# Decode attention with a gated unit on one core: keys and probabilities turned by VectorE instead of TensorE, softmax per key tile

## The chip, the cores and the metric

The kernel runs on 1 core of a Trainium2 chip. The metric is the device time of one execution in microseconds (us), lower is better. The engines named below are PE (TensorE: matmuls; PEld is its weight load), DVE (VectorE), ACT (ScalarE), POOL (GpSimd) and SP (SyncE, which here only issues DMAs).

## The reference

One decoding step of a block for 8 sequences (B = 8, one token each, D = 512). All tensors are bf16.

```python
xn = layernorm(x)                                   # 8 x 512
q  = (xn @ wq) -> 32 heads of 128
k  = k_cache[:, :, 8192-2048:, :]                   # 8 kv heads, window W = 2048
v  = v_cache[:, :, 8192-2048:, :]                   # each kv head serves 4 query heads
s  = softmax(q . k * 128**-0.5) . v   -> 8 x 4096,  then @ wo   -> 8 x 512
g  = silu((sigmoid(xn @ w_gate) * (xn @ w_up)) @ w_down)        # F = 1792
out = x + s * g
```

The window of keys and values is 2 x 32 MB, the weights are some 14 MB: 81 MB to read.

## The kernel before

**Tiles and loads.** A key or value tile holds 4 kv heads of one sequence: 128 partitions x 64 positions x 128 numbers, 2 MB. Each partition holds 64 neighbouring positions of one head, and the partitions go round the four heads (partition 4p + l has head l). There are 16 key tiles and 16 value tiles (sequence b, half i of the heads). All loads go through SP's queue in a fixed list: the weights of the gated unit and wq, then key tile n and value tile n - 3 in turn, at last wo in five pieces. `pump` issues the next load of the list as soon as its pool (`room`: 5 key buffers, 4 value buffers) has room in the program's order; SP itself waits until the buffer's last reader is done. wq and wo use key buffers, the gated unit's weights value buffers.

**Before the loop.** Layernorm, the gated unit's two products, q (`q_ps` L344), the gated unit's last product, and some selector tiles built from identities by POOL and DVE. `qm_sb` holds q turned, 4 query rows of one kv head in 32 columns that are otherwise zero; `M0` and the offset `o` in `scores` shift them so that one head's scores land on rows of their own.

**The loop**, over sequences b and 16 half steps s each, an order written out by hand (`tasks`): `k_transposes` (L488) turns the keys 128x128 at a time by matmuls with a permutation, which also sorts the heads, into PSUM, 16 to a group, and DVE copies each group to SBUF (L493, kT_sb). `scores` (L505) multiplies four heads side by side, each in its own 32 columns of the PE array. Once for a sequence, one step behind: `row_max`, `stat_rows`, `spread_max` find the maximum of each head over its rows (a DVE maximum, a PE transpose to one row, two small DVE operations, a PE transpose back) and take the exponentials into `p_buf`; `p_transposes` (L599) turns the probabilities on PE and DVE copies them (L590). Two sequences behind, `values` (L625) multiplies them with the value tiles; `combine`, `heads`, `divide` merge the parts of each head and divide by the sums.

**The tail.** The last two sequences' probabilities and values, then the product with wo (`part_ps` L754, `fin_ps` L768), the gate, the sum with x, and the store.

Of the kernel before, what the change touches and what calls it, by code (L numbers as in the profile page):

```python
# [10 lines left out]
def kernel(  # L11
# [13 lines left out]
    nc = tc.nc  # L25
# [17 lines left out]
    CH = CU // 2  # L43
    NU = NQ * NJ
    NR = NU * rep
# [9 lines left out]

    padpool = ctx.enter_context(tc.tile_pool(name="padpool", bufs=1))
    padpool.tile([P, 96], f32, name="pad")
    kpool = ctx.enter_context(tc.tile_pool(name="kpool", bufs=5))
    vpool = ctx.enter_context(tc.tile_pool(name="vpool", bufs=4))
    ktpool = ctx.enter_context(tc.tile_pool(name="ktpool", bufs=3))  # L60
    ppool = ctx.enter_context(tc.tile_pool(name="ppool", bufs=2))
# [23 lines left out]
    room = {"k": 5, "v": 4, "d": 1}  # L85
# [127 lines left out]
    for t0, t1 in ((0, 12), (12, KS), (KS, 26), (26, 30), (30, RT)):  # L213
        want_rows("wo_sb", A_wo, "k", RT, t0, t1)

    pump()

    perm = consts.tile([P, P], bf16, name="perm")
    nc.gpsimd.tensor_copy(
        out=perm[:].rearrange("k (l p) -> k l p", l=G),  # L220
        in_=ident[:].rearrange("k (p l) -> k l p", l=G),
    )

# [34 lines left out]
    M0 = Z - rep  # L258
    qm_sb = work.tile([P, B, Hkv, M0 + Z], bf16, name="qm_sb")
    nc.gpsimd.memzero(qm_sb[:])  # L260
    p_buf = [work.tile([P, PG, G, CU], bf16, name=f"p_buf{i}") for i in range(2)]
    for t in p_buf:
        nc.gpsimd.memzero(t[:])
# [75 lines left out]
    q_ps = [ps_s.tile([P, rep * Dh], f32, name="q_ps", tag="s") for _ in range(2)]  # L339
    for kt in range(KT):  # L340
        for x in range(Hkv // JQ):
            for j in range(JQ):
                g = x * JQ + j
                nc.tensor.matmul(  # L344
                    q_ps[x][Z * j : Z * (j + 1), :],
                    lhsT=xnT_sb[:, kt, :],
                    rhs=weights[("wq_sb", kt)][:, g * rep * Dh : (g + 1) * rep * Dh],
                    start=(kt == 0),
                    stop=(kt == KT - 1),
                    tile_position=(0, Z * j),  # L350
                    skip_group_check=True,
                )
    q_bf = ktpool.tile([P, 2, rep, Dh], bf16, name="q_bf", tag="kT")
    qT_ps = ps_t.tile([P, 2, rep, P], bf16, name="qT_ps", tag="t")
    for x in range(Hkv // JQ):
        src = q_ps[x][:].rearrange("k (r d) -> k r d", r=rep)
        nc.scalar.copy(out=q_bf[:, x], in_=src)
    for x in range(Hkv // JQ):
        for r in range(rep):
            nc.tensor.transpose(  # L360
                out=qT_ps[:, x, r, :], in_=q_bf[:, x, r, :], identity=ident[:]
            )
        nc.vector.tensor_copy(  # L363
            out=qm_sb[:, :, x * JQ : (x + 1) * JQ, M0 : M0 + rep],
            in_=qT_ps[:, x].rearrange("d r (j z) -> d z j r", z=Z)[:, ::S],
        )
# [25 lines left out]
    w_ps = ps_s.tile([P, D], f32, name="w_ps", tag="s")  # L392
# [13 lines left out]
    b_ps = ps_s.tile([P, P], f32, name="b_ps", tag="s")  # L406
# [16 lines left out]
    Hh = G * rep  # L423
    turn_rows = consts.tile([P, P], bf16, name="turn_rows")
    sel_den = consts.tile([P, Hq], f32, name="sel_den")
    sel_out = consts.tile([P, 2, Hq], f32, name="sel_out")
    for i in range(NQ):
        nc.gpsimd.tensor_copy(
            out=turn_rows[:].rearrange("k (i j l r) -> k i j l r", i=NQ, j=NJ, l=G)[
                :, i  # L430
            ],
            in_=ident[:].rearrange("k (l j i r) -> k i j l r", i=NQ, j=NJ, l=G)[:, i],
        )
        nc.vector.reduce_sum(
            out=sel_den[:, i * Hh : (i + 1) * Hh].rearrange("k (l r) -> k l r", l=G),
            in_=ident_f[:].rearrange("k (l j i r) -> k i l r j", l=G, j=NJ, i=NQ)[:, i],
            axis=AX.X,
        )
    for e in range(2):
# [19 lines left out]
    sel_sum = consts.tile([P, Hq, NDQ], f32, name="sel_sum")  # L459
    nc.gpsimd.tensor_copy(  # L460
        out=sel_sum[:], in_=sel_den[:].unsqueeze(2).to_broadcast([P, Hq, NDQ])
    )
# [8 lines left out]
    kT_ps = {}  # L471
# [10 lines left out]
    def k_transposes(b, u, h):  # L482
        i, j = u // NJ, u % NJ
        k_sb = k_tiles[(b, i)]
        if h == 0:
            kT_ps[0] = ps_t.tile([P, CU, P], bf16, name="kT_ps", tag="t")
        for c in range(h * CH, (h + 1) * CH):
            nc.tensor.transpose(  # L488
                out=kT_ps[0][:, c, :], in_=k_sb[:, j * CU + c, :], identity=perm[:]
            )  # L490
        if h == 1:
            kT[(b, u)] = ktpool.tile([P, CU, P], bf16, name="kT_sb", tag="kT")
            nc.vector.tensor_copy(out=kT[(b, u)][:], in_=kT_ps.pop(0)[:])  # L493
        if j == NJ - 1 and h == 1:
            del k_tiles[(b, i)]
            free("k")

    def scores(b, u):
        i, j = u // NJ, u % NJ
        if u == 0:  # L500
            s_ps[b] = ps_s.tile([P, CU * PG], f32, name="s_ps", tag="s")
        t = kT.pop((b, u))
        o = M0 - rep * (j * NQ + i)
        for l in range(G):
            nc.tensor.matmul(  # L505
                s_ps[b][NR * l : NR * (l + 1), :],
                lhsT=qm_sb[:, b, i * G + l, o : o + Z],
                rhs=t[:, :, PG * l : PG * (l + 1)],
                start=(u == 0),
                stop=(u == NU - 1),  # L510
                tile_position=(0, NR * l),
                skip_group_check=True,
            )


    NH = NQ * rep

    def row_max(b):
        st[b] = small.tile([P, 1], f32, name="st")
        nc.vector.reduce_max(out=st[b][:], in_=s_ps[b][:], axis=AX.X)  # L520

    def stat_rows(b):
        nc.tensor.transpose(out=r_ps[b % 2], in_=st.pop(b)[:], identity=ident_f[:])
        top = small.tile([1, G, NH], f32, name="top")
        nc.vector.reduce_max(
            out=top[:],
            in_=r_ps[b % 2].rearrange("o (l j h) -> o l h j", l=G, j=NJ),
            axis=AX.X,
        )
        row[b] = small.tile([1, G, NJ, NH], f32, name="neg")  # L530
        nc.vector.tensor_scalar(
            out=row[b][:],
            in0=top[:].unsqueeze(2).to_broadcast([1, G, NJ, NH]),
# [5 lines left out]
    def spread_max(b):  # L539
        nc.tensor.transpose(  # L540
            out=nb_ps[b % 2],
            in_=row.pop(b)[:].rearrange("o l j h -> o (l j h)"),
# [3 lines left out]
        nc.scalar.copy(out=nb[:], in_=nb_ps[b % 2])  # L546

        s = s_ps.pop(b)
        if b % 2 == 0:
            sums_of[b // 2] = small.tile([P, 2], f32, name="sums")  # L550
        if b == B - 1:
            e_sb = ktpool.tile([P, PG, CU], bf16, name="e_sb", tag="kT")
            nc.scalar.activation(  # L553
                out=e_sb[:],
                in_=s[:].rearrange("k (c p) -> k p c", p=PG),
                func=AF.Exp,
                bias=nb[:],
                scale=scale,
                accum_out=sums_of[b // 2][:, b % 2 : b % 2 + 1],
            )  # L560
            move = (
                nc.vector.tensor_copy,
                nc.gpsimd.tensor_copy,
                nc.scalar.copy,
                nc.vector.tensor_copy,
            )
            for l in range(G):
                rows = slice(NR * l, NR * (l + 1))
                move[l](out=p_buf[b % 2][rows, :, l, :], in_=e_sb[rows])  # L569
            return  # L570
        for l in range(G):
            rows = slice(NR * l, NR * (l + 1))
            nc.scalar.activation(  # L573
                out=p_buf[b % 2][rows, :, l, :],
                in_=s[rows, :].rearrange("k (c p) -> k p c", p=PG),
                func=AF.Exp,
                bias=nb[rows, :],
                scale=scale,
                accum_out=sums_of[b // 2][rows, b % 2 : b % 2 + 1],
            )  # L580

    pT_ps = {}

    def p_transposes(b):
        p_turn(b, 0)
        p_turn(b, 1)
        p_copy(b, 0, CU, nc.vector.tensor_copy)

    def p_copy(b, c0, c1, copy):
        copy(out=pT[b][:, c0:c1, :], in_=pT_ps[b][:, c0:c1, :])  # L590
        if c1 == CU:
            del pT_ps[b]

    def p_turn(b, h):
        if h == 0:
            pT[b] = ppool.tile([P, CU, P], bf16, name="pT_sb")
            pT_ps[b] = ps_t.tile([P, CU, P], bf16, name="pT_ps", tag="t")
        for c in range(h * CH, (h + 1) * CH):
            nc.tensor.transpose(  # L599
                out=pT_ps[b][:, c, :],  # L600
                in_=p_buf[b % 2][:, :, :, c].rearrange("k p l -> k (p l)"),
                identity=turn_rows[:],
            )


# [214 lines left out]
```

## Time and profile before

| what | value |
|---|---|
| median of 3 runs | 199.63 us (199.42 to 200.01) |
| profiled execution | 199.11 us, its span 197.3 us |
| granted PE clock, mean over the span | 0.972 |
| DMA | 81.32 MB, mean 412 GB/s, 16 engines busy at 9 tenths or more from the second slice to the last but two |
| key transposes L488 on PE | x1024, 76.5 us |
| their copies L493 on DVE | x64, 78.2 us, mean 1222 ns |
| value matmuls L625 | x512, 38.7 us |
| score matmuls L505 | x256, 25.9 us |
| exponentials L573 on ACT | x28, 19.0 us, mean 679 ns, each with an accumulator read of 184 ns |

The profile is of one execution. Its span runs from the first to the last instruction, and the execution took 1.8 us more. Busy times of PE are modelled at their ends, since matmuls are pipelined. The chain that ended last is followed back from the last instruction to what released each step.

### The profile page before, as it was taken

The page shows a single profiled execution, that of the slowest core. Times are in us where ns is not written, and L with a number is a line of the kernel's source. Part 1 is how long each engine was busy: PE and PEld are TensorE (multiplying, and loading weights), DVE is VectorE, ACT ScalarE, POOL GpSimd, SP SyncE. Part 2 cuts the span into 40 slices and gives each one's busy share as a digit, 9 for nine tenths or more (in the row PEclk, how much of TensorE's full clock was granted, in tenths as well). Part 3 has the DMA queues.
Part 4 walks back from the last instruction along what each step waited for, and adds up shares of the span by engine and source line. Part 5 has one row for each costly group of instructions (what it writes and reads, how often), then busy time and mean ns, then how long its engine had stood idle before and what let it go on. Part 6 is the DMA issues. An engine that isn't in the chain of part 4 may idle for free.

```text
span 197.3 us, 4706 instructions
## 1 busy us (share of the span) xinstructions
PE 155.2 (79%) x2138; PEld 105.4 (53%) x2138; DVE 114.9 (58%) x144; ACT 35.8 (18%) x87; POOL 13.8 (7%) x32
## 2 busy tenths in 40 slices
PE   0073575999799996999798979796989797749763
PEld 0021124777586675667565746474658464538521
DVE  4624002889877574657794766476848664764311
ACT  0510210000900600060006001500050024032110
POOL 8960001000000000000000000000000000010000
PEclk9999999999999998899999999999999999999975
DMA  6999999999999999999999999999999999999980
GB/s 212 436 438 438 423 431 422 432 435 425 428 428 435 423 428 428 442 422 425 425 432 423 432 432 425 435 428 428 432 428 425 425 428 432 438 428 424 407 372 29
DMA packets 6436, 81.32 MB, mean 412 GB/s; under 512 B 777, under 2 KB 785, under 8 KB 1553
## 3 DMA queue, kind: packets, MB, share of 16 engines
q1 hardware_dynamic: 6237, 80.10, 95.3%
q10 hardware_dynamic: 180, 0.93, 1.4%
q8 instruction: 16, 0.26, 0.5%
q14 instruction: 3, 0.02, 0.0%
HBM read 81.02 MB, written 0.01 MB: 411 GB/s over the span
## 4 chain that ended last, share of the span: by engine, by line
DMA 75%; PE 20%; SPq 1%; DVE 1%; issue 0%; ACT 0%; DVEq 0%
DMA k_sb<-in_A_k_cache_dram 62%; PE kT_ps L488 11%; DMA wo_sb<-in_A_wo_dram 10%; PE o_ps L625 4%; DMA wg_sb<-in_B_w_gate_dram 3%; PE s_ps L505 3%; PE fin_ps L768 1%; PE pT_ps L599 1%; SPq L90 1%; DVE kT_sb L493 1%; PE part_ps L754 1%; ACT part L764 0%; SPq L100 0%; SPq L150 0%; DVE prod L783 0%
## 5 line engine op out<-in xcount | busy, mean ns | idle before, releaser
L493 DVE COPY kT_sb<-kT_ps 128x2048 bf16<-128x2048 bf16 x64 | 78.2, 1222 | 37.0 <-PE kT_ps L488 36.6
L488 PE MATMUL kT_ps<-perm,k_sb 128*128 128x128 bf16 x1024 | 76.5, 225 | 12.3 <-DMA k_sb<-in_A_k_cache_dram 12.2
L488 PEld LDWEIGHTS <-k_sb 128*128 128x128 bf16 x1024 | 60.5, 100 | 32.5 <-issue 16.3
L625 PE MATMUL o_ps<-v_sb,pT_sb 128*32 128x256 bf16 x512 | 38.7, 276 | 2.3 <-DVE pT_sb L590 2.3
L625 PEld LDWEIGHTS <-pT_sb 128*32 128x32 bf16 x512 | 21.6, 96 | 10.8 <-DVE pT_sb L590 2.7
L505 PE MATMUL s_ps<-kT_sb,qm_sb 128*32 128x512 bf16 x256 | 25.9, 393 | 1.4 <-DVE kT_sb L493 1.2
L573 ACT ACTIVATE p_buf<-s_ps,nb 32x512 bf16<-32x512 f32 x28 | 19.0, 679 | 0.5
L546 ACT COPY nb<-m_ps 128x1 f32<-128x1 f32 x8 | 1.3, 159 | 91.9 <-PE m_ps L540 91.9
L590 DVE COPY pT_sb<-pT_ps 128x2048 bf16<-128x2048 bf16 (+1 forms) x8 | 9.3, 1158 | 5.0 <-PE pT_ps L599 5.0
L505 PEld LDWEIGHTS <-qm_sb 128*32 128x32 bf16 x256 | 7.4, 93 | 8.3 <-issue 1.9
L599 PE MATMUL pT_ps<-turn_rows,p_buf 128*128 128x128 bf16 x128 | 9.9, 229 | 1.1 <-ACT p_buf L573 1.1
L569 POOL COPY p_buf<-e_sb 32x512 bf16<-32x512 bf16 x1 | 0.7, 667 | 143.1 <-ACT e_sb L553 143.1
L599 PEld LDWEIGHTS <-p_buf 128*128 128x128 bf16 x128 | 8.8, 150 | 3.0 <-issue 1.6
L641 ACT ACTIVATE o_odd<-o_ps,own_col 128x128 f32<-128x128 f32 x8 | 2.9, 367 | 29.6 <-PE o_ps L625 29.6
L248 PE MATMUL xnT_ps<-ident,xn_bf 8*128 8x8 bf16 x4 | 0.3, 174 | 10.1 <-DVE xn_bf L237 10.1
L344 PE MATMUL q_ps<-wq_sb,xnT_sb 128*32 128x512 bf16 x32 | 3.8, 625 | 5.7 <-DMA wq_sb<-in_A_wq_dram 5.7
L520 DVE TENSOR_REDUCE st<-s_ps 128x1 f32<-128x512 f32 x8 | 5.4, 680 | 0.5 <-PE s_ps L505 0.5
L248 PEld LDWEIGHTS <-xn_bf 8*128 8x128 bf16 x4 | 0.2, 114 | 10.1 <-DVE xn_bf L237 10.1
L344 PEld LDWEIGHTS <-xnT_sb 128*32 128x32 bf16 x32 | 1.3, 130 | 8.1 <-issue 8.1
L363 DVE COPY qm_sb<-qT_ps 128x128 bf16<-128x128 bf16 x2 | 0.6, 292 | 8.2 <-PE qT_ps L360 8.2
L674 DVE SCALAR_TENSOR_TENSOR own<-m_ps,inv,own_q 128x128 f32<-128x128 f32 x8 | 2.8, 347 | 4.2 <-PE m_ps L664 4.2
L573 ACT ACTIVATION_READ_ACCUMULATOR p_buf<-s_ps,nb 32x1 f32 x28 | 5.1, 184 | 0.0
(86 smaller groups left out, 76.5 us busy)
## 6 DMA issues: line engine op xcount, KB each, us to landing
k_sb<-in_A_k_cache_dram SPq DMA_DIRECT2D x16, 2048.0 KB, 31.2
v_sb<-in_A_v_cache_dram SPq DMA_DIRECT2D x16, 2048.0 KB, 27.3
wq_sb<-in_A_wq_dram SPq DMA_DIRECT2D x2, 2048.0 KB, 16.7
wu_sb<-in_B_w_up_dram SPq DMA_DIRECT2D x1, 1792.0 KB, 10.2
wd_sb<-in_B_w_down_dram SPq DMA_DIRECT2D x1, 1536.0 KB
wo_sb<-in_A_wo_dram SPq DMA_DIRECT2D x1, 1536.0 KB, 18.3
wo_sb<-in_A_wo_dram SPq DMA_DIRECT2D x1, 1024.0 KB
wg_sb<-in_B_w_gate_dram ACTq DMA_DIRECT2D x1, 896.0 KB
```

What stands on the lines that cost most here:

```text
L90: q0.dma_start(out=t[:].rearrange("p c d -> p (c d)"), in_=cache[b, G * i : G * (i + 1), win0:Sk, :].rearrange("l (p c) d -> p l (c d)", c ...
L344: nc.tensor.matmul(q_ps[x][Z * j : Z * (j + 1), :], lhsT=xnT_sb[:, kt, :], rhs=weights[("wq_sb", kt)][:, g * rep * Dh : (g + 1) * rep * Dh ...
L488: nc.tensor.transpose(out=kT_ps[0][:, c, :], in_=k_sb[:, j * CU + c, :], identity=perm[:])
L493: nc.vector.tensor_copy(out=kT[(b, u)][:], in_=kT_ps.pop(0)[:])
L505: nc.tensor.matmul(s_ps[b][NR * l : NR * (l + 1), :], lhsT=qm_sb[:, b, i * G + l, o : o + Z], rhs=t[:, :, PG * l : PG * (l + 1)], start=(u ...
L520: nc.vector.reduce_max(out=st[b][:], in_=s_ps[b][:], axis=AX.X)
L573: nc.scalar.activation(out=p_buf[b % 2][rows, :, l, :], in_=s[rows, :].rearrange("k (c p) -> k p c", p=PG), func=AF.Exp, bias=nb[rows, :], ...
L590: copy(out=pT[b][:, c0:c1, :], in_=pT_ps[b][:, c0:c1, :])
L599: nc.tensor.transpose(out=pT_ps[b][:, c, :], in_=p_buf[b % 2][:, :, :, c].rearrange("k p l -> k (p l)"), identity=turn_rows[:],)
L625: nc.tensor.matmul(o_at[b][rows].rearrange("k (e d) -> k e d", e=2), lhsT=pT[b][:, c, rows], rhs=v[:, m, c], start=(c == 0), stop=(c == CU ...
L641: nc.scalar.mul(out=o_odd[:], in_=o_at[b][:, Dh:], mul=own_col[:, 1:2])
L674: nc.vector.scalar_tensor_tensor(out=own[:], in0=m_ps[:, b % 2, P : 2 * P].rearrange("p (q t) -> p q t", q=NDQ), scalar=inv[b // 2][:, b % ...
```

## The change

- **Keys** are turned by DVE (`turn_keys`): one instruction turns half a key tile as 32x32 blocks of 4-byte elements, that is of pairs of bf16 numbers, from SBUF to SBUF. PE's transposes, their PSUM and the copies go. A block turns 32 partitions (8 groups of positions of each of the four heads) by 32 pairs. After it, each of the four groups of 32 partitions has 32 pairs of numbers, with keys of all four heads in its columns, and a matmul contracts the even or the odd members of 32 pairs.
- **Queries** are laid out block-diagonally for it: `q_bf` repeats each part of q four times, 32 small matmuls turn it, and four copies (DVE and ACT in turn) put the 16 queries of the four heads block by block on the four groups of partitions in `qm_sb`.
- **Scores** (`scores(t, m)`) of half a tile are nine matmuls of 128 rows by 512 columns into one PSUM bank: one with `mask_rows` and `mask_cols` adds -2^100 where a row and a column belong to different heads, eight accumulate q . k. The exponential of a masked score is zero.
- **Softmax** runs for each of the 16 key tiles instead of for each of the 8 sequences: `row_max` over 1024 columns, two exponentials of 128 x 512 for a tile.
- **Probabilities** are turned by DVE too (`turn_p`, 512 elements of 4 bytes), SBUF to SBUF. The zeros of the foreign heads let `values` multiply with all four heads' value rows at once. `sums` becomes four matmuls.
- **Order**: one step for a key tile, written out below. `values` runs three tiles behind. The kT pool has 2 buffers instead of 3, the key pool 4 instead of 5, and the last piece of wo uses a value buffer.

```diff
-    kpool = ctx.enter_context(tc.tile_pool(name="kpool", bufs=5))
+    kpool = ctx.enter_context(tc.tile_pool(name="kpool", bufs=4))
-    ktpool = ctx.enter_context(tc.tile_pool(name="ktpool", bufs=3))
-    ppool = ctx.enter_context(tc.tile_pool(name="ppool", bufs=2))
+    ktpool = ctx.enter_context(tc.tile_pool(name="ktpool", bufs=KB))    # KB = 2
+    ppool = ctx.enter_context(tc.tile_pool(name="ppool", bufs=3))
...
-    perm = consts.tile([P, P], bf16, name="perm")
-    nc.gpsimd.tensor_copy(...)
...
-    qm_sb = work.tile([P, B, Hkv, M0 + Z], bf16, name="qm_sb")
+    qm_sb = work.tile([P, NQ * NJE, B, GR + P], bf16, name="qm_sb")
     nc.gpsimd.memzero(qm_sb[:])
-    for t in p_buf:
-        nc.gpsimd.memzero(t[:])
+    mask_rows = consts.tile([G, P // GR, G, rep], bf16, name="mask_rows")
+    mask_cols = consts.tile([G, CU * PS, G], bf16, name="mask_cols")
...
     for x in range(Hkv // JQ):
-        nc.scalar.copy(out=q_bf[:, x], in_=src)
+        (nc.scalar.copy, nc.vector.tensor_copy)[x](
+            out=q_bf[:, x], in_=q_ps[:, x] ... .to_broadcast([P, rep * NJE // NE, NE, QS, PG]))
+    for x in range(Hkv // JQ):
+        for y in range(NJE):
+            for r in range(rep):
+                nc.tensor.matmul(qT_ps[:, x, y, r] ..., lhsT=q_bf[...], rhs=ident[:, ::S], ...)
+    for s in range(QS):
+        (nc.vector.tensor_copy, nc.scalar.copy)[s % 2](
+            out=qm_sb[rows, :, :, o : o + GR] ..., in_=qT_ps[rows] ...)
...
+    def turn_keys(t, m):
+        k_sb = k_tiles[order[t]]
+        kT[(t, m)] = ktpool.tile([P, NJE // NE, CM, PG, NE], bf16, name="kT_sb", tag="kT")
+        nc.vector.transpose(
+            out=kT[(t, m)][:].rearrange("k y c p e -> k c y (p e)").bitcast(f32),
+            in_=k_sb[:, CM * m : CM * (m + 1), :]
+            .rearrange("k c (y d) -> k c y d", y=NJE // NE).bitcast(f32))
+        if m == NM - 1:
+            free("k")
+    def scores(t, m):
+        nc.tensor.matmul(s_ps[t][:, m], lhsT=mask_rows, rhs=mask_cols, start=True, stop=False)
+        for e in range(2):
+            for y in range(NJE):
+                nc.tensor.matmul(
+                    s_ps[t][:, m],
+                    lhsT=qm_sb[:, i * NJE + y, b, GR * (1 - e) : GR * (1 - e) + P],
+                    rhs=keys[:, y // NE, CU * e : CU * (e + 1), :, y % NE], ...)
...
+    def turn_p(t):
+        pT[t] = ppool.tile([P, NM * CU // 2, NX, 2], bf16, name="pT_sb")
+        nc.vector.transpose(out=pT[t] as f32, in_=p_buf[t % 2] as f32)
...
+    for t in range(NT):
+        pv = t - AHEAD                       # AHEAD = 3
+        turn_keys(t, 0)
+        if t >= 1:
+            turn_p(t - 1)
+        scores(t, 0)
+        turn_keys(t, 1)
+        if t >= 5 and t % 2 == 1:
+            combine((t - 5) // 2)
+        scores(t, 1)
+        if t >= 8 and t % 4 == 0:
+            normalise((t - 8) // 2, (t - 8) // 2 + 2)
+        if t % 4 == 1 and t >= 5:
+            sums((t - 5) // 4)
+        if pv >= 0:
+            values(pv, 0, CH)
+        row_max(t)
+        stat_rows(t)
+        if pv >= 0:
+            values(pv, CH, CU)
+        spread_max(t)
+
+    turn_p(NT - 1)
     heads(B - 4, B - 2)
     divide(B - 4)
     divide(B - 3)
+    values(NT - 3, 0, CU)
     combine(B - 2)
+    values(NT - 2, 0, CU)
     sums(B // 2 - 1)
     heads(B - 2, B - 1)
     divide(B - 2)
+    values(NT - 1, 0, CU)
     combine(B - 1)
     normalise(B - 1, B)
```

## The prediction

> **What bounds the kernel now.** I read the 40 slices first, then the chain that ended last, then stretches and the timeline.
>
> ```profile
> PE 155.2 (79%) x2138; PEld 105.4 (53%) x2138; DVE 114.9 (58%) x144; ACT 35.8 (18%) x87; POOL 13.8 (7%) x32
> ...
> DMA  6999999999999999999999999999999999999980
> ...
> DMA 75%; PE 20%; SPq 1%; DVE 1%; issue 0%; ACT 0%; DVEq 0%
> ```
>
> From 5 to 190 us the DMA engines never pause. The chain, in order of time, ends so:
>
> ```profile
> 169.75 20.05 DMA wo_sb<-in_A_wo_dram
> 189.80 0.04 issue
> 189.84 1.07 PE part_ps L754 x8
> ```
>
> The last weights land at 189.8, and only the tail follows. The bytes stay the same, so nothing can be gained before 189.8. The change can only keep up with a key and a value tile (4.19 MB, 9.75 us at 430 GB/s) per step, or fall behind.
>
> Now PE bears the turning (1024 transposes, 76.5 us) and VectorE only copies. This stretch of the last softmax gives what one costs in order:
>
> ```profile
> 172.63 0.69 DVE L520 TENSOR_REDUCE st<-s_ps 128x1 f32<-128x512 f32 x1 [0.50 <-PE s_ps L505]
> ...
> 173.69 0.28 DVE L525 TENSOR_REDUCE top<-m_ps 1x32 f32<-1x128 f32 x1 [0.36 <-PE m_ps L523]
> 174.00 0.21 DVE L531 TENSOR_SCALAR neg<-top 1x128 f32<-1x128 f32 x1
> ...
> 174.53 0.16 ACT L546 COPY nb<-m_ps 128x1 f32<-128x1 f32 x1 [5.63 <-PE m_ps L540]
> 174.72 0.69 ACT L553 ACTIVATE e_sb<-s_ps,nb 128x512 bf16<-128x512 f32 x1
> ```
>
> It runs 8 times now, beside PE's own work; after the change it runs 16 times, and VectorE stands in it.
>
> **Price of the new operations.** The only transpose on VectorE now is
>
> ```profile
> 16.25 0.65 DVE L333 STREAM_TRANSPOSE hT_sb<-h_sb 128x448 bf16<-128x448 bf16 x1
> ```
>
> 448 elements at 0.96 per ns (the slope by which the 512-element reduction takes 0.68) are 0.47, so 0.18 is fixed. A key transpose has 2048 elements of 4 bytes: 2.31 us if elements count; 4.45 if bytes count (8192 against 896 in that row). Below: 1.22, the copy of 2048 2-byte elements at L493 (mean 1222 ns). I take 2.31, since the row is the same operation. The Trainium skill, Vector Engine (DVE) Microarchitecture Reference, section 3.8, says the turning array sustains one element per cycle per lane; by it the 4.45 falls away, but no run here shows it for 4 bytes. The turn of probabilities (512 elements) is 0.72.
>
> Score matmuls become 128x128 by 512 columns. No row has that; value matmuls (L625) run 32 in 1.92 us, two at a time, so 0.109 per 256 columns after 0.17 of drain: 0.218 per 512. Above: 0.277 (L754, three waves in 0.83) and 0.33 to 0.40 (L505's waves). The moving operand now reads every second element of a key tile, and could cost up to that. I take 0.218, the nearest in what PE does: long rows, one behind the other.
>
> **One step (tile t), in VectorE's order.** Two key turns with their gaps 2.35 + 2.34; between them turn_p(t-1), 0.75, which waits for the exponentials. After the second turn PE needs 8 matmuls: 0.05 + 1.75 + 0.17 = 1.97, and VectorE stands in row_max(t). Behind it in VectorE's queue are the two small operations and the next tile's key turns, so the wait is paid in every step, and SP's next k_sb waits for those turns. The maximum over 1024 columns: 0.68 + 0.53 + 0.04 = 1.25. Then PE's transpose and the two small operations, as above from 173.32 to 174.21: 0.89. Sum 9.55. The exponentials start behind 16 value matmuls (0.93) and spread_max: 1.65 after the maximum, and two take 1.57 (0.78 each with its accumulator read), so they end 3.22 after it; VectorE is back from its next key turn at 0.89 + 2.35 = 3.24. So turn_p waits for nothing, barely. The mask matmul, first half's scores and value matmuls lie in PE's idle time at 0.22, 1.75 and 0.06 each and cost nothing here; uncovered, they would cost 3.9 a step.
>
> Steps: 16 x 9.55 = 152.8. Extra, where PE does something between the scores and row_max and VectorE stands behind it: sums at t = 5, 9, 13 (four float32 matmuls, the row at 183.53 has 0.38 for one, some 0.3 each in a stream, and the reciprocal with its wait 0.3) 3 x 1.5 = 4.5; normalise at 8 and 12 (heads 0.7, two divides of 0.35 + 0.39) 2 x 2.1 = 4.2. The exponential's table load (1.28) delays step 1 by 1.0. combine lies in the wait for scores: nothing.
>
> **PE's clock.**
>
> ```profile
> 73.50:77.00 3.50, 1.88 (x29) 1.40 (x26) 2.63 (x4) 0.00 (x0) 0.00 (x0) 0.99 0.98 421
> 77.00:80.40 3.40, 3.40 (x33) 2.46 (x31) 1.73 (x2) 0.00 (x0) 0.00 (x0) 0.50 1.01 434
> 80.40:83.80 3.40, 3.40 (x51) 2.20 (x49) 1.81 (x4) 0.00 (x0) 0.00 (x0) 1.00 1.03 439
> ```
>
> (PE busy is the second number, granted clock the third from the end.) After a stretch with PE busy 54% the clock was 0.50 for the next 3.4 us, and full again after one busy stretch. The first three steps hold no value matmuls: 18 x 0.218 in 9.55 is 41%, so part of them runs at half clock. Then the second half's scores queue behind the first's (17 matmuls of 0.43 in a row), and a step is 2.4 longer: 0 to 7.3 in all, I take 3.7. From t = 3 it is 60%, and by the places of its pieces no 3.4 us of it is under about 52%: full clock. (That the bound lies between is an estimate from the stretch above and from 172.5 to 176, which had 2.42 of 3.45 busy and kept the clock.) The Trainium skill, TensorE: Matmul & The Clock Gate, section "Why this matters for your kernels", asks only for no idle gap over about 3 us; by that the 3.7 is nothing and the sum 221.8. The trace speaks against it: the gap before 76.8 was 1.6 us.
>
> **Start.** Now K's first transpose starts at 32.3, when the tile lands, and everything before it is done. After: q matmuls end at 23.5 as now. q_bf is four times as wide and its two copies wait for each other (ScalarE 1.95 by L590's 1012 ns for 1024; VectorE 2.28), 27.8. 32 instead of 8 matmuls, half of them behind the second copy, 30.0. The four qm copies of 1024 columns alternate between engines, each waiting: 1.2 + 1.1 + 1.2 + 1.1, 34.6. Behind them on ScalarE hP_sb (0.36), then eight matmuls at half clock (1.1), w_sb 0.58, b_ps 0.7, sigb 0.3, and on VectorE gg_sb 0.3 and the selectors' reductions 0.8: turn_keys(0, 0) starts at 39.0, 6.7 after the tile. Bounds: 36 (no mutual waits) and 41. GpSimd's larger memset (4608 for 1920 words, +2.4) and the mask tiles end before q, and its perm copy (2.56) and p_buf memsets (1.83) go: nothing.
>
> **Sum.** 39.0 + 152.8 + 4.5 + 4.2 + 1.0 + 3.7 = 205.2 to the last row maximum. Then PE, in order: rest of the step 0.4, heads 0.5, values of tiles 13 and 14 1.9 each, sums 1.4, heads 0.5, values of 15 1.9, and drain, combine, heads, divide 2.3 (183.5 to 188.7 shows them): 10.8. Then, as from 188.7 to 197.3 now less the wait: 7.7. Span 223.7; the profiled execution took 199.1 for a span of 197.3, so 1.8 more: **225.5**. (The runs' median, 199.63, is 0.5 above that execution.)
>
> The queue: SP waits for v buffers, V15's for tile 11's values in step 14 (195.7), with the wo loads behind it. V15 lands about 202, wo (4 MB) by 212, before their matmuls at 216. So DMA stops being the end; four key buffers instead of five cost nothing: each is free some 8 us before DMA comes to it at first, and later the v buffers are the later ones.
>
> **Rivals.**
> - PE takes longer per score matmul (strided reads or half clock throughout). At 0.277: +0.47 a step, 234. At 0.33: 243. At half clock, 0.427, PE's two halves become the step: 11.9 x 16, about 267. For: L505's waves; against: the value matmuls' rate. 0.16.
> - Not slower: the key turns take two elements a cycle, 1.22. Then turn_p waits 1.1 for the exponentials, a step is 8.5, under the DMA's 9.75, and with half the extras hidden the last wo at 189.8 sets the end again: 198 to 202, 200 likeliest. It decides from a turn under about 1.2. For: L493 moves two elements a cycle, though 2-byte ones; against: L333 at one. The Trainium skill, VectorE: DVE Perf Modes, section "The perf-mode tier table", gives float32 copies in SBUF two a cycle but does not list the transpose. 0.08.
> - Bytes count, 4.45: a step 13.9, about 294. 0.05.
>
> **Numbers.** Forecast 0.71 (its own range 212 to 233: the start's and clock's bounds and 0.3 a step). The range 208 to 246 adds the near part of the first rival. No change means within 0.3% (0.6 us), which the runs' own spread (199.42 to 200.01) about equals. Not slower comes only from the second rival, half of it: faster 0.04 (full clock in the tail could save 1), same 0.04, slower 0.92.
>
> **What would show it.** Right: VectorE transposes of 2.3 us x32; PE's waits on them; row_max's wait on s_ps about 2 a step; DMA share under 9 in the later slices; the last v_sb issues waiting for o_ps; steps 9.5 apart. Wrong: a transpose under 1.3 or over 3; scores over 0.25 apart; DMA still solid to 190; turn_p's wait over 1 us a step.

## The result, and the profile after

The changed kernel takes 224.97 us (median of 4 runs, 221.73 to 227.19) against 199.56 us (199.42 to 200.01) before. The ratio is 1.1137, with a 95% interval of 1.1077 to 1.1196; it rests on the two shorter runs (mean 222.3), which the comparisons below use too, since the two of 227 us are in a slower state whose cause no run shows. The profiled execution took 222.93 us for a span of 221.2.

From the page of the changed kernel, the busy times, the granted clock and the DMA share by slices (one slice is 5.53 us), the chain that ended last, and four groups:

```profile
PE 145.7 (66%) x1082; PEld 66.5 (30%) x1082; DVE 133.0 (60%) x142; ACT 38.4 (17%) x100; POOL 12.2 (5%) x30
...
PEclk9997555585879699999999799999969678879999
DMA  6999999999999999999999999999997634569920
...
PE 45%; DVE 34%; DMA 9%; ACT 8%; issue 2%; SPq 1%; ACTq 0%
...
L543 PE MATMUL s_ps<-kT_sb,qm_sb 128*128 128x512 bf16 x256 | 78.2, 457 | 30.5 <-DVE kT_sb L517 30.5
L517 DVE STREAM_TRANSPOSE kT_sb<-k_sb 128x2048 f32<-128x2048 f32 x32 | 72.9, 2280 | 0.0
L553 DVE TENSOR_REDUCE st<-s_ps 128x1 f32<-128x1024 f32 x16 | 19.5, 1220 | 28.6 <-PE s_ps L543 28.6
...
L598 DVE STREAM_TRANSPOSE pT_sb<-p_buf 128x512 f32<-128x512 f32 x16 | 11.3, 704 | 4.0 <-ACT p_buf L587 3.3
```

No engine is full: PE is busy 66% of the span, VectorE 60%. Yet the chain, 75% DMA before, is now 45% PE and 34% VectorE. The two wait for each other: PE 30.5 us for turned keys, VectorE 28.6 us for scores, in 11 of the 16 steps (in the other five the wait ends with the sums or the heads instead). The DMA row is solid only to the 30th slice, about 166 us, and then falls to 3 to 7 tenths for six slices. The waits of SP's queue (engine and line, what it waited for, us in total, times, longest) show what the loads stood behind:

```profile
SPq L93 <- PE m_ps L576: 75.2, 12, 11.5
SPq L93 <- DVE kT_sb L517: 56.2, 8, 11.7
SPq L93 <- DVE o_sb L644: 17.5, 4, 4.4
```

That is PE's order and VectorE's key turns, so the steps. (SP waited for buffers in the kernel before as well, 85.9 us for L488 and 36.0 us for L625 on PE, but the DMA never fell idle there.) One ordinary step, t = 7, in the timeline (start, duration, engine and line; in brackets the wait ahead of it), from its first key turn to the next tile's:

```profile
109.83 2.29 DVE L517 STREAM_TRANSPOSE kT_sb<-k_sb 128x2048 f32<-128x2048 f32 x1
...
112.18 0.71 DVE L598 STREAM_TRANSPOSE pT_sb<-p_buf 128x512 f32<-128x512 f32 x1
112.18 1.97 PE L543 MATMUL s_ps<-kT_sb,qm_sb 128*128 128x512 bf16 x8 [1.47 <-DVE kT_sb L517]
112.81 2.27 DVE L517 STREAM_TRANSPOSE kT_sb<-k_sb 128x2048 f32<-128x2048 f32 x1
...
115.14 1.96 PE L543 MATMUL s_ps<-kT_sb,qm_sb 128*128 128x512 bf16 x8 [0.67 <-DVE kT_sb L517]
117.14 1.23 DVE L553 TENSOR_REDUCE st<-s_ps 128x1 f32<-128x1024 f32 x1 [1.82 <-PE s_ps L543]
118.42 0.27 PE L558 MATMUL m_ps<-ident_f,st 128*1 128x128 f32 x1 [0.34 <-DVE st L553]
118.72 0.28 DVE L560 TENSOR_REDUCE top<-m_ps 1x16 f32<-1x128 f32 x1 [0.36 <-PE m_ps L558]
119.03 0.21 DVE L566 TENSOR_SCALAR neg<-top 1x128 f32<-1x128 f32 x1
119.18 2.29 DVE L517 STREAM_TRANSPOSE kT_sb<-k_sb 128x2048 f32<-128x2048 f32 x1
```

It is one chain through VectorE's queue: turn, turn probabilities, turn, stand 1.82 us for eight score matmuls, maximum, its two small operations, next turn: 9.35 us. From one step's maximum to the next, the steps at full clock take 9.32 to 9.45 us.

What the forecast did not have is in the stretches that follow (length, then PE busy; the granted clock is third from the end):

```profile
117.99:121.40 3.41, 1.73 (x21) 1.05 (x20) 3.01 (x4) 1.52 (x5) 0.00 (x0) 1.00 1.01 428
121.40:124.82 3.42, 3.30 (x8) 0.97 (x7) 2.98 (x3) 0.09 (x2) 0.00 (x0) 0.50 1.01 431
124.82:128.20 3.38, 3.38 (x24) 1.70 (x25) 0.45 (x2) 0.00 (x0) 0.00 (x0) 1.00 1.00 422
```

PE is busy 1.73 of 3.41 us, 51%, and runs the next stretch at half clock. There, in step t = 8, the first half's eight score matmuls take 3.50 us instead of 1.97. That step takes 11.9 us; most of the excess is its `normalise`, since the same step takes 11.1 us at full clock (second experiment).

### The profile page after: what moved, and what is told of

The parts are those of the page before. It is cut to its first block, busy times and chain, and to the rows that moved or that the text cites. A ratio compares the mean times of both kernels' runs of the same rounds, so it can differ in the third digit from the quotient of the medians.

```text
span 221.2 us, 2591 instructions
## 1 busy us (share of the span) xinstructions
PE 145.7 (66%) x1082; PEld 66.5 (30%) x1082; DVE 133.0 (60%) x142; ACT 38.4 (17%) x100; POOL 12.2 (5%) x30
## 4 chain that ended last, share of the span: by engine, by line
PE 45%; DVE 34%; DMA 9%; ACT 8%; issue 2%; SPq 1%; ACTq 0%
PE s_ps L543 29%; DVE kT_sb L517 16%; DVE st L553 9%; DMA wq_sb<-in_A_wq_dram 9%; PE o_ps L623 6%; ACT p_buf L587 5%; DVE pT_sb L598 2%; PE m_ps L558 2%; PE s_ps L533 2%; PE m_ps L607 2%; PE m_ps L662 1%; DVE qm_sb L400 1%; DVE top L560 1%; DVE q_bf L378 1%; ACT qm_sb L400 1%
## 5 line engine op out<-in xcount | busy, mean ns | idle before, releaser
L543 PE MATMUL s_ps<-kT_sb,qm_sb 128*128 128x512 bf16 x256 | 78.2, 457 | 30.5 <-DVE kT_sb L517 30.5
L517 DVE STREAM_TRANSPOSE kT_sb<-k_sb 128x2048 f32<-128x2048 f32 x32 | 72.9, 2280 | 0.0
L543 PEld LDWEIGHTS <-qm_sb 128*128 128x128 bf16 x256 | 26.7, 107 | 72.8 <-issue 55.8
L553 DVE TENSOR_REDUCE st<-s_ps 128x1 f32<-128x1024 f32 x16 | 19.5, 1220 | 28.6 <-PE s_ps L543 28.6
L623 PE MATMUL o_ps<-v_sb,pT_sb 128*32 128x256 bf16 x512 | 32.5, 274 | 0.0
L587 ACT ACTIVATE p_buf<-s_ps,nb 128x512 bf16<-128x512 f32 x32 | 21.7, 683 | 0.5
L533 PE MATMUL s_ps<-mask_cols,mask_rows 4*128 4x512 bf16 x32 | 13.8, 431 | 0.0
L598 DVE STREAM_TRANSPOSE pT_sb<-p_buf 128x512 f32<-128x512 f32 x16 | 11.3, 704 | 4.0 <-ACT p_buf L587 3.3
L228 DVE CAST x_f<-x_bf 8x512 f32<-8x512 bf16 x1 | 5.3, 5304 | 2.7 <-DMA x_bf<-in_A_x_dram 2.7
L587 ACT ACTIVATION_READ_ACCUMULATOR p_buf<-s_ps,nb 128x1 f32 x32 | 6.3, 196 | 0.0
## 6 DMA issues: line engine op xcount, KB each, us to landing
wu_sb<-in_B_w_up_dram SPq DMA_DIRECT2D x1, 1792.0 KB, 10.4
wo_sb<-in_A_wo_dram SPq DMA_DIRECT2D x1, 1536.0 KB, 11.9
```

Source lines behind the costliest of these rows:

```text
L228: nc.vector.tensor_copy(out=x_f[:], in_=x_bf[:])
L517: nc.vector.transpose(out=kT[(t, m)][:] .rearrange("k y c p e -> k c y (p e)") .bitcast(f32), in_=k_sb[:, CM * m : CM * (m + 1), :] .rearr ...
L533: nc.tensor.matmul(s_ps[t][:, m], lhsT=mask_rows[:].rearrange("k x l r -> k (x l r)"), rhs=mask_cols[:].rearrange("k c l -> k (c l)"), sta ...
L543: nc.tensor.matmul(s_ps[t][:, m], lhsT=qm_sb[:, i * NJE + y, b, GR * (1 - e) : GR * (1 - e) + P], rhs=keys[:, y // NE, CU * e : CU * (e + ...
L553: nc.vector.reduce_max(out=st[t][:], in_=s_ps[t][:].rearrange("k m c -> k (m c)"), axis=AX.X)
L587: nc.scalar.activation(out=p_buf[t % 2][:, m * CU // 2 : (m + 1) * CU // 2], in_=s[:, m].rearrange("k (c e p) -> k c p e", e=2, p=PG), fun ...
```

## The experiments

The theory: **VectorE's serial order** sets the step (a wait inside it, not VectorE's amount of work), and **half-clock stretches** come on top. The rivals: VectorE simply has too much to do; PE or its strided reads are the bound; or the shortage of key buffers holds back the loads. All runs are of one core.

**The maximum moved behind the next tile's first key turn.** The part `row_max`, `stat_rows`, `spread_max` of a tile runs one key turn later, and `turn_p` one later too. VectorE does the same operations in another order. PE's order changes a little with it: a tile's values come in one piece, and the second half's scores stand behind `normalise` and `sums`.

```diff
         turn_keys(t, 0)
         if t >= 1:
-            turn_p(t - 1)
+            row_max(t - 1)
+            stat_rows(t - 1)
+            spread_max(t - 1)
         scores(t, 0)
         turn_keys(t, 1)
...
+        if t >= 1:
+            turn_p(t - 1)
...
+        scores(t, 1)
         if pv >= 0:
-            values(pv, 0, CH)
-        row_max(t)
-        stat_rows(t)
-        if pv >= 0:
-            values(pv, CH, CU)
-        spread_max(t)
+            values(pv, 0, CU)
+    row_max(NT - 1)
+    stat_rows(NT - 1)
+    spread_max(NT - 1)
     turn_p(NT - 1)
```

> Same work in another order: the maximum, its two small operations and the exponentials of tile t-1 stand behind the first key turn of tile t, so VectorE never waits for scores it has just made possible. My theory (VectorE standing in row_max while PE makes the scores, some 2 us of a step of 9.4, is what puts the step over the DMA's 9.75 together with the extras and the late start): VectorE's step falls to 2.33 + 1.27 + 0.86 + 2.30 + 0.75 = 7.5 us, DMA is solid again to about 190 us, time 199 to 203. Rival A (PE's score matmuls or its clock are the bound): 215 or more. Rival B (four key buffers or the value buffers hold the DMA up by themselves): DMA still has gaps before 190, time over 206.

Measured: 198.93 us (198.84 to 198.98, 6 runs), 0.9957 of the kernel before (0.9934 to 0.998): all the loss is gone, and the time is a hair under the expected 199 to 203. Its page shows the DMA solid to the end again, VectorE with the same 32 turns, but now waiting for loads, not for scores:

```profile
DMA  6999999999999999999999999999999999999980
...
L517 DVE STREAM_TRANSPOSE kT_sb<-k_sb 128x2048 f32<-128x2048 f32 x32 | 73.3, 2293 | 11.8 <-DMA k_sb<-in_A_k_cache_dram 10.0
```

A step of it in VectorE's timeline (from one tile's first turn at 107.87 to the next's at 115.50), and a later one:

```profile
107.87 2.30 DVE L517 STREAM_TRANSPOSE kT_sb<-k_sb 128x2048 f32<-128x2048 f32 x1
110.10 1.18 DVE L553 TENSOR_REDUCE st<-s_ps 128x1 f32<-128x1024 f32 x1
...
112.10 2.29 DVE L517 STREAM_TRANSPOSE kT_sb<-k_sb 128x2048 f32<-128x2048 f32 x1
...
114.68 0.70 DVE L598 STREAM_TRANSPOSE pT_sb<-p_buf 128x512 f32<-128x512 f32 x1
115.50 2.29 DVE L517 STREAM_TRANSPOSE kT_sb<-k_sb 128x2048 f32<-128x2048 f32 x1
...
154.37 2.31 DVE L517 STREAM_TRANSPOSE kT_sb<-k_sb 128x2048 f32<-128x2048 f32 x1 [2.02 <-DMA k_sb<-in_A_k_cache_dram]
156.61 1.19 DVE L553 TENSOR_REDUCE st<-s_ps 128x1 f32<-128x1024 f32 x1
```

The maximum starts without a wait, because PE multiplied while VectorE turned the next half tile. VectorE's waits for scores fall from 28.6 to 3.0 us in all. A step is 7.1 to 8.5 us until VectorE has caught up with the loads, and then 9.63 to 9.78 for five steps: the pace of a key and a value tile, which the prediction put at 9.75. So the amount of VectorE's work was never the bound, and the order was. The clock matters no more: the profiled run has half clock at 49.4, 66.4, 131.3 and from 158.6 to 165.4 us inside the loop, and the DMA row stays solid.

**PE kept busy.** The changed kernel with unused matmuls of 512 columns in PE's idle places: three behind the first half's scores, five at a step's end (nine while there are no values yet), five more in the steps with `normalise`.

```diff
+    def fill(n):
+        for _ in range(n):
+            nc.tensor.matmul(fill_ps[:], lhsT=ident[:], rhs=qm_sb[:, 0, 0:4, 0:P], ...)
...
         scores(t, 0)
+        fill(3)
...
+        if t >= 8 and t % 4 == 0:
+            fill(5)
         row_max(t)
...
         spread_max(t)
+        fill(5 if pv >= 0 else 9)
```

> Adds matmuls of 512 columns that nothing uses (3 between the two halves' scores, 5 at the end of a step, 9 in the first three steps, 5 more in the steps with a normalise) so that PE has no half idle stretch. By the steps of the changed kernel's profile (16 steps take 166 us; at 9.4 with 1.0 for the table load, 0.8 for each sums and 2.0 for each normalise they would take 158) the half clock costs about 8 us. Theory: granted clock near 1.0 from the second step on, time about 217 (215 to 219). Rival (the clock costs nothing because VectorE's chain hides it, or the added matmuls delay as much as they save): 224 or more.

Measured: 217.32 us (216.87 to 218.97), 1.0905 of before (1.0859 to 1.0951). PE has more work, and the time is 5.0 us under the changed kernel's 222.3: within the expected range, though the half clock was expected to cost about 8. The same stretch of this kernel, and then of the changed one:

```profile
70.50:119.20 48.70, 45.75 (x315) 21.72 (x314) 35.23 (x34) 8.84 (x29) 0.00 (x0) 1.00 1.01 429
```

```profile
70.50:119.20 48.70, 36.20 (x264) 17.44 (x266) 34.66 (x35) 8.56 (x27) 0.00 (x0) 0.96 1.01 421
```

The clock is full from 46 to 209 us, and the steps that were at full clock before take the same 9.32 to 9.44, so the added matmuls delay nothing there. From the maximum of t = 3 to that of t = 15 the steps take 118.7 us in sum against 123.6 in the profiled execution of the changed kernel. So half clock from t = 3 on costs that execution 4.8 us, and 17.6 us of the loss against before remain with PE filled.

**An extra turn inside the wait, and the same on the path.** One more VectorE transpose of 512 elements per step (0.70 us), whose output nobody reads: once between the second key turn and the maximum, once behind `stat_rows`.

```diff
         turn_keys(t, 1)
...
+        nc.vector.transpose(out=junk[:], in_=extra_in[:])
         scores(t, 1)
```

> Adds one turn of 512 elements on VectorE (0.71 us, result unused) in each step between the second key turn and row_max, where VectorE waits about 2 us for the scores. Theory: hidden, 0 to +1 us on the kernel after the change (224 to 227). Rival (VectorE's busy time as such is the bound): +11.8.

```diff
         row_max(t)
         stat_rows(t)
+        nc.vector.transpose(out=junk[:], in_=extra_in[:])
```

> The same added turn, but between the small operations of the maximum and the next tile's first key turn, where VectorE waits for nothing. Theory: on the path, 16 x 0.74 = +11.8 us less what turn_p's wait for the exponentials gives back (0.1 to 0.2 a step): +8 to +12, 233 to 238. Rival (PE or the exponentials end the step): under +3.

Inside the wait: 226.42 us. Its runs (219.21, 226.23, 226.61, 226.89) stand against 221.73, 222.93, 227.0 and 227.19 of the changed kernel: neither the shortest nor the longest is longer, but four runs spread so wide give no interval. On the path: 238.09 (237.59 to 240.44), 1.1954 of before (1.1893 to 1.2015) and 15.8 above the changed kernel's 222.3. The same 0.70 us, 16 times, costs nothing that the runs tell apart in the one place and some 16 us in the other. The timelines show it in step t = 6, at full clock in all three kernels. In the first kernel the maximum still waits 1.47 us for scores behind the extra turn (2.05 in the changed kernel), so the turn lies in the wait:

```profile
105.30 0.67 DVE L692 STREAM_TRANSPOSE junk<-extra_in 128x512 f32<-128x512 f32 x1
107.44 1.23 DVE L555 TENSOR_REDUCE st<-s_ps 128x1 f32<-128x1024 f32 x1 [1.47 <-PE s_ps L545]
```

In the second it pushes the key turn behind it (this is the next turn, of t = 7):

```profile
113.99 0.69 DVE L692 STREAM_TRANSPOSE junk<-extra_in 128x512 f32<-128x512 f32 x1
114.62 2.26 DVE L519 STREAM_TRANSPOSE kT_sb<-k_sb 128x2048 f32<-128x2048 f32 x1
```

From the maximum of t = 5 to that of t = 6 it is 9.33 in the first kernel, 9.32 in the changed one, and 9.75 in the second: 0.43 more, though the key turn starts 0.63 later; part of it is given back in shorter gaps (from a key turn's start to `turn_p` it is 2.19 us there, 2.35 before). That makes 16 x 0.43 = 6.9 us, under the expected 8 to 12. The rest, some 9 us, is longer steps, 10.6 to 13.7 us, with stretches at half clock in them, which the expectation left out.

**Four key buffers in the kernel before**, the last piece of wo in a value buffer, as the change has them.

```diff
-    kpool = ctx.enter_context(tc.tile_pool(name="kpool", bufs=5))
+    kpool = ctx.enter_context(tc.tile_pool(name="kpool", bufs=4))
...
-    room = {"k": 5, "v": 4, "d": 1}
+    room = {"k": 4, "v": 4, "d": 1}
```

> The kernel before with the change's loads alone: four key buffers instead of five, and the last piece of wo in a value buffer. Theory: a buffer fewer costs nothing, DMA stays solid to 190, 199 to 200. Rival (part of the loss is the missing key buffer): over 202.

Measured: 199.47 us, 0.9994 of before (0.9976 to 1.0012). The fifth buffer is worth nothing there.

**The start.** The kernel with PE filled, and in it the two turns of tile 0 ahead of the gated unit's last product, with a buffer of its own for `w_sb`.

```diff
+    turn_keys(0, 0)
+    turn_keys(0, 1)
     down = [(hT_sb[:, t, :], weights[("wd_sb", t)]) for t in range(SD, FT)]
...
-    w_sb = ktpool.tile([P, 2, 512], f32, name="w_sb", tag="kT")
+    w_sb = work.tile([P, 1, 512], f32, name="w_sb")
```

> The kernel with PE filled (e2_pe_filled, 217.3), and the two key turns of tile 0 moved ahead of the gated unit's last product in VectorE's order, with w_sb in a buffer of its own: they can begin at 32.3, when tile 0 has landed and VectorE's last qm copy ends, instead of 38.2. The first scores then stand behind b_ps on PE at 36.8 and the first maximum comes some 3.4 us earlier. Theory (the steps run one behind the other from the first turn on, so a late start is paid once and in full): 213 to 215. Rival (the start is hidden, because the end is set by loads or by the values): 216.5 or more.

Measured: 214.29 us (213.4 to 215.45), 1.0732 of before (1.0689 to 1.0774), 3.0 less than with PE filled alone. The timeline:

```profile
32.25 4.50 DVE L415 STREAM_TRANSPOSE kT_sb<-k_sb 128x2048 f32<-128x2048 f32 x2 [0.22 <-DMA k_sb<-in_A_k_cache_dram]
42.90 1.22 DVE L557 TENSOR_REDUCE st<-s_ps 128x1 f32<-128x1024 f32 x1 [4.95 <-PE s_ps L547]
```

The turns start 5.9 us earlier, the first maximum 5.0 (47.89 with PE filled), and the last maximum 2.6 (193.7 against 196.29). The difference of 2.4 is lost in two early steps that fell into half-clock stretches (11.16 and 11.26 against 10.33 and 9.66). So the late start does reach the end; that it does so in full, as expected, the time alone does not show.

**Keys read without a step.** With PE filled, the score matmuls read 512 neighbouring elements instead of every second one, so each multiplies a mixture of the keys' numbers.

```diff
-                    rhs=keys[:, y // NE, CU * e : CU * (e + 1), :, y % NE],
+                    rhs=keys[:, y // NE, 8 * (2 * e + y % NE) : 8 * (2 * e + y % NE) + 8],
```

> The kernel with PE filled, but the score matmuls read 512 neighbouring elements of the turned keys instead of every second one, so they multiply the wrong numbers; sizes and counts stay. Theory (the step of two costs nothing, 0.2255 us from one to the next is what a row of 512 takes): same spacing, same time, 216 to 219. Rival (the step costs): spacing 0.214 or less, and 1 to 2 us off.

Measured: 219.39 us in one run, against 216.87 to 218.97 with PE filled. In the middle of the run the matmuls follow one another at 0.2155 us instead of 0.226, and a step is 0.08 shorter. So the strided read has a price, against my expectation, but some 1.3 us in all (16 x 0.08, an estimate); the single time does not show it, since two early steps fell into half-clock stretches (11.1 us).

**The tail of the reordered kernel.** Twice I put unused matmuls into the tail of the first experiment's kernel, to have the last products at full clock (4, 4, 5 and 3 of them; then 4, 5, 3, 3, 4 and 2 in other places).

> The kernel with the maximum later (e1_max_later, 198.93, DMA solid to 190), and matmuls that nothing uses in PE's waits after the last values, so that its clock is not halved when the last weights land: in e1's profile the clock is half from 189 on, eight part_ps matmuls take 1.05 us and the fin_ps ones 0.66 and 1.96, where the kernel after the change, at full clock, took 0.43 and 0.85. Theory: the end after the last landing is 1 to 1.5 us shorter, 197.4 to 198.2. Rival (the added matmuls are themselves late, or the clock falls all the same): 198.8 or more.

> The kernel with the maximum later, and the unused matmuls placed anew: in e7 PE had stood idle ahead of the last value tile, so the clock fell before the values (3.16 us for 32 instead of 1.93) and the added matmuls, at half clock, held up part_ps. Now 4 stand ahead of the last sums, 5 ahead of the last values, 3 behind them and 3 behind heads, 4 ahead of the eight part_ps matmuls that wait for the last weights, 2 ahead of fin_ps. Theory: full clock from the last values to the end, part_ps and fin_ps as after the change (0.43 and 0.85 for fin_ps), 197.6 to 198.4, so about 0.8 under e1's 198.93. Rival (the clock falls in one of the windows all the same): 198.7 or more.

Measured: 198.88 us, 0.9955 of before (0.9943 to 0.9968), and 198.9, 0.9985 (0.997 to 1.0): no gain on the 198.93, and both expectations missed. The second had the clock full from the last steps to 195 us, and its timeline shows what then sets the end:

```profile
192.84 0.41 PE L767 MATMUL fin_ps<-wo_sb,oP_sb 128*32 128x128 bf16 x16 [0.71 <-DMA wo_sb<-in_A_wo_dram]
193.48 0.29 PE L767 MATMUL fin_ps<-wo_sb,oP_sb 128*32 128x128 bf16 x8 [0.23 <-DMA wo_sb<-in_A_wo_dram]
```

The last matmuls wait for the last pieces of wo, which land at about 193.4. The half clock in the tail lay beside the DMA's work. Why the reordered kernel is a few tenths under the kernel before (spans 197.1 and 197.3) isn't settled: no run takes that difference apart, and the three ratios reach from 0.9955 to 0.9985.

## Why the prediction was right, and where it was not

The forecast was 225.5 us (span 223.7), the chances 0.92 for slower. Measured: 224.97 over all runs, 222.93 in the profiled execution with a span of 221.2. No single run took 225, so the half microsecond to the median says little; the profiled execution, on whose terms the forecast was built, was 2.6 shorter. The mechanism is as told, and both ends of it were tested: the order is the cause (the reordered kernel), VectorE's wait has room (the extra turn in it) and the rest of its path has none (the extra turn on it). By the sum's own stages, in the profiled execution:

| term | predicted | measured |
|---|---|---|
| first key turn starts | 39.0 | 38.15 |
| 16 ordinary steps | 152.8 | 150.2 (16 x 9.39, the mean of the full-clock steps) |
| sums and normalise | 8.7 | 6.05 (3 x 0.85 + 2 x 1.75, from the steps with PE filled) |
| table load and half clock, first three steps | 4.7 | 4.2 |
| half clock later | 0 | 5.7 (what is left to 204.3; 4.8 of it from t = 3's maximum on) |
| last row maximum and its two small operations done | 205.2 | 204.3 |
| to the last oP, then to the end | 10.8 + 7.7 | 10.4 + 6.5 |

- **The key turn** was predicted at 2.31 and takes 2.28. The three rows it was chosen from (1.22, 2.31, 4.45) were far apart, and the row of the same operation at another size was the right one. Twice the bytes at the same number of elements cost nothing, which is what the Trainium skill, Vector Engine (DVE) Microarchitecture Reference, section 3.8, says of the turning array (one element per cycle per lane); the 2.28 us for 2048 elements of 4 bytes agree.
- **The score matmul** was put at 0.218 and is 0.226. The rival that PE takes 0.277 or more falls. At half clock it is 0.427, as that rival had it, but only in some stretches, not throughout. (Its prices don't follow from the step alone: 8 x 0.112 more a step gives 240 at 0.33, not 243, and a step of 11.9 gives 263, not 267.)
- **The step** was 0.16 too long, mostly in gaps between VectorE's operations: the two key turns with `turn_p` between them take 5.25 us where the sum had 5.44. `turn_p` waits for the exponentials twice only, in step 1 (1.04 us) and behind the last step (2.27). An ordinary step of 9.39 would even keep up with the loads' 9.75; the 16 steps take 166 us, 10.4 each, only with the rows of the table that follow it, and they start late. The reordered kernel's 7.1 to 8.5 leave room for both.
- **Sums and normalise** were each over-priced, at 1.5 and 2.1 against 0.85 and 1.75. At t = 5 the four float32 matmuls of the sums hold PE for 0.87 us (97.31 to 98.18) where the sum had 1.2, and the reciprocal delays the maximum by 0.09 (98.29 to 98.38) where it had 0.3. In normalise the heads take 0.52 (125.22 to 125.74 with PE filled) for 0.7 and the divides 1.34 (125.85 to 127.19) for 1.48.
- **The step that failed is the clock from t = 3.** The prediction had full clock there, since by the places of PE's work no 3.4 us of a step would be busy under about 52%. By its own anchors (54% losing the clock, 70% keeping it) that was not enough to conclude it. And the ordinary steps fall lower: PE is busy 1.64 us of the 3.41 from 79.60 to 83.01, and 1.68 from 108.60 to 112.01, 48% and 49%. The clock stayed full in and behind those two, and fell behind others. The half-clock stretches of this trace start at 49.7, 63.4, 73.6, 121.4, 162.4, 172.6, 186.3 and 196.5 us, always whole multiples of 3.413 us apart, and last one or two such lengths. That fits a clock set length by length on a fixed grid of time, across which the steps of 9.3 to 12 us drift, so that only some of the poor stretches meet it; no run tests this. Nor does the busy share alone decide. The two anchors leave out a stretch of the kernel before, busy 48% (first line) and followed by full clock (second line):

```profile
175.95:179.40 3.45, 1.65 (x26) 1.39 (x27) 1.71 (x2) 0.19 (x1) 0.34 (x1) 1.00 1.02 437
179.40:182.80 3.40, 3.40 (x79) 3.14 (x79) 2.16 (x6) 1.38 (x2) 0.00 (x0) 1.00 1.00 426
```

In the changed kernel the stretch from 128.20 to 131.60, on the same grid, is busy 51% like the one at 117.99, and the clock stayed. What decides is open. With PE filled the term vanishes. That the forecast came near all the same is luck: the other terms were over-priced by 8.2 together, against the 5.7 that the clock took, which leaves the span 2.5 too long.
- **The Trainium skill's rule on the clock**, TensorE: Matmul & The Clock Gate, section "Why this matters for your kernels", asks for no idle gap over about 3 us. Keeping to it was not enough here: the stretch at 117.99 has 1.68 us of idle time in all, so no gap of it was longer, and the next stretch ran at half clock.
- **The last loads.** The DMA row ends in the 39th slice, at some 211.5 us (predicted 212), wo's matmuls do not wait for it any more, as predicted, and the four key buffers cost nothing, which the run on the kernel before confirms. What the prediction read amiss is the kernel before: the weights' end was taken as 189.8, from one step of the chain. The DMA share of that kernel is still 0.57 between 192 and 193 us, and the second tail run shows the last pieces at about 193.4. A version that keeps up with the DMA and has these loads last can therefore hardly end before that, whatever its clock is.

## What to carry to other kernels

When work moves from one engine to another and neither becomes full, look at the queue of the engine that gets it: an operation that waits for another engine holds up everything queued behind it. Put independent work of the next tile ahead of it; here the new order, with the same operations, was worth 23 us (222.3 to 198.93). Price a clock that depends on PE's idle time over the whole run, not over one typical step.

## What the runs showed of the hardware that I had not expected

- A VectorE transpose of 2048 4-byte elements takes 2.28 us and one of 512 takes 0.70: 1.03 ns per element and 0.18 fixed. The bf16 row of before (448 in 0.65) lies on the same line, so bf16 numbers moved in pairs cost half per number.
- A stretch of 3.41 us with PE busy 51% was followed by one at half clock, another with 51% and one with 48% by full clock. Half-clock stretches of one execution start whole multiples of 3.413 us apart and last one or more such lengths. One with PE busy 97% was followed by full clock, but in the reordered kernel one with 95% (158.56 to 161.97) by another at half clock.
- With PE filled, the run with a mean clock of 0.928 took 218.97 us and those at 0.999 took 216.87 and 217.04. In the first, half clock lies from 18.7 to 46.0 us, ahead of the loop's first maximum, and twice behind 209 us; of the others no trace is kept.
- A moving operand of bf16 read with a step of two costs 0.226 us per 512 columns against 0.2155 without.
